# Attention and gated convolutional MLP on one core: the MLP starts two steps earlier, three weight pieces are converted beside it

## The chip, the cores and the metric

The kernel runs on one core of a Trainium2 chip. The time is that of one execution on the device in microseconds (us); a kernel's time is the median of its runs. The profile is one further execution, recorded by the hardware profiler. TensorE (PE) multiplies matrices, VectorE (DVE) and ScalarE (ACT) work elementwise and may read the accumulators in PSUM, GpSimd (POOL) works elementwise on SBUF alone, SyncE (SP) issues nearly all DMAs. Each engine takes its instructions in the order in which they stand.

## The reference, cut to what matters

```python
# q, k, v: (4, 8, 576, 64) float32; x after it: (4, 576, 512)
q_rot, k_rot = rotate(q), rotate(k)                 # rotary embedding
scores = scale * np.matmul(q_rot, k_rot.transpose(0, 1, 3, 2))
scores = scores - np.max(scores, axis=-1, keepdims=True)
attn = np.exp(scores)
attn = attn / (np.sum(attn, axis=-1, keepdims=True) + 1e-09)
x = heads side by side of np.matmul(attn, v)
h = np.maximum(x @ w_in, 0.0)                       # w_in (512, 1024) float64
conv_out[s] = conv_w[0] * h[s-1] + conv_w[1] * h[s] + conv_w[2] * h[s+1]
out = (h / (1 + np.exp(-conv_out))) @ w_out         # w_out (1024, 512) float64
```

## The kernel before

There are 16 pairs of heads (4 batches by 4 pairs) with five steps each (`STEPS`): pair p has the steps 5p to 5p+4, one for each block of 128 queries, the fifth for the 64 queries left over. For one step, written in this text as letters:

- **S**: the scores of 128 queries on PE (`emit_S`, L251), then two row maxima on DVE (L259) and two exponentials with their sums on ACT (L263).
- **T**: 16 transposes of the exponentials on PE (`emit_T`, L311), taken out of PSUM by two copies on ACT into `pt` (L189). **R** is the transpose of the last 128 keys (`emit_Trem`, L336), taken out by ACT or DVE (`evac`, L189 or L191). S4 and T4 are S and T of the fifth step, which is half as much work.
- **E**: once per pair and half of the sequence, 20 matmuls of `pt` with v on PE (`emit_E`, L367); ACT copies the result (L377), DVE multiplies by the reciprocal sums (L381), ACT and POOL split it into a high and a low part `xT` (L385, L386).

The MLP (MoE in the code) works on eight blocks of 288 tokens, two for each batch. **M1** (`emit_M1`, L400) is one of eight units per block, 12 matmuls of `xT` with the split weights `winh` and `winl` in PSUM tile `pm`; after it come relu on ACT (L408), three taps of the convolution (L412 and twice L414 on DVE), tanh on ACT (L420), the gate on DVE (L423), and the split into `g` on ACT and POOL (L431, L432). These follow their M1 after 2, 5, 7 and 9 ticks (`defer`, `tick`); a tick goes by after most PE units. **M2** (`emit_M2`, L478) is a quarter of the down projection of 128 tokens, six matmuls of `g` with `wouth` and `woutl`. M1 of a block needs `xT` of all four pairs of its batch, M2 needs `g`.

The weights arrive as float64 in 16 pieces of 128 by 512 (`load_w`, 512 KB each) and become two float32 parts (`conv_w_piece`, `to_f32`): absolute value on ACT (L496), clamp, shift, merge and sign on DVE (L499, L505, L508, L513), the high part on ACT (L556), the low part by four subtractions on POOL (L559). The rotary embedding runs on POOL (`rope`, L180 and L183), for q and k of each pair nine instructions each, and DVE turns its result into `qT` and `kT` (L224, L227).

Nothing is scheduled by a planner at run time: `emit` fills a table (`plan`) of steps and ranks by `at(step, rank, fn)` and another (`moe`) of MLP units per step, and then emits both step by step. `WIDE` is the step at which the MLP begins; before it the steps use the wide PSUM layout of three banks per score tile and no MLP tiles, and all weight pieces are spread evenly over them. At `WIDE` the pools change, and block 0 begins; blocks take `MB` = 10 steps each, with `room` as the share of a step that is given to them. After step 79 the attention is over; the last two blocks run in a tail of their own.

Of the kernel before, what the change touches and what calls it, by code (L numbers as in the profile page):

```python
# [20 lines left out]
def attention_moe_kernel(ctx, tc, q, k, v, w_in, conv_w, w_out, tab, tabx, out):  # L21
# [52 lines left out]
    late = {"tail": False, "short": False}  # L74
# [257 lines left out]
    def emit_Trem(p, first, num):  # L332
        ps = spare(128 * num)
        for u in range(num):
            x = ST[p, first + u].rearrange("p h k -> p (h k)")[:, 512:640]
            nc.tensor.transpose(ps[:, 128 * u:128 * u + 128], x, idf)  # L336
        after(lambda: evac("V", pt[:, 8, 128 * first:128 * (first + num)], ps))
# [52 lines left out]
    def emit_M1(blk, f):  # L390
# [18 lines left out]
        c = late["pc"].tile([128, HS], F32, tag="c", name="c")  # L409

        def conv():
            nc.vector.tensor_scalar(out=c, in0=r[:, j:j + HS], scalar1=cw[:, f:f + 1], scalar2=None, op0=ALU.mult)  # L412
            for e in (1, 2):
                nc.vector.scalar_tensor_tensor(  # L414
                    out=c, in0=r[:, j + e:j + e + HS], scalar=cw[:, 8 * e + f:8 * e + f + 1], in1=c,
                    op0=ALU.mult, op1=ALU.add,
                )
# [72 lines left out]
    def to_f32(pool, w64, w, n):  # L490
        w32 = w64.bitcast(I32).rearrange("p (n t) -> p n t", t=2)
        h, l = w32[:, :, 1], w32[:, :, 0]
        t = pool.tile([128, n], I32, tag="wt", name="wt", bufs=3)[0:w64.shape[0]]
# [23 lines left out]
        return first, clamp, second, third  # L517
# [11 lines left out]
    def load_w(i):  # L529
        if i >= len(WPIECES):  # L530
            return
        src, _, _, kk, c = WPIECES[i]
        t = late["ws"].tile([128, 512], I64, tag="w64", name="w64", bufs=4)
        nc.sync.dma_start(out=t, in_=src[kk * 128:kk * 128 + 128, c:c + 512])
        stage[i] = t

    def conv_w_piece(i):
# [3 lines left out]
        def first():  # L541
            box["w"] = late["ws"].tile([128, 512], F32, tag="wf", name="wf", bufs=3)
            box["s"] = to_f32(late["ws"], stage.pop(i), box["w"], 512)
            box["s"][0]()
# [5 lines left out]
        def third():  # L550
            box["s"][3]()
            load_w(i + 3)
# [18 lines left out]
    def conv_cw():  # L571
        t = stage.pop("cw")
        w = late["ws"].tile([32, 128], F32, tag="cwf", name="cwf", bufs=1)
        for fn in to_f32(late["ws"], t, w, 128):
            fn()
        stage["cwf"] = w
# [9 lines left out]

    late["ws"] = wctx.enter_context(tc.tile_pool(name="ws", bufs=2))
    wcv = [conv_w_piece(i) for i in range(len(WPIECES))]
    wsteps = [wcv[0][0]]
    for i in range(len(wcv)):  # L590
        wsteps += [wcv[i + 1][0]] if i + 1 < len(wcv) else []
        wsteps += wcv[i][1:]

    WIDE = 26
# [8 lines left out]
    def emit():  # L603
        with tc.manual_schedule(engines=engines):
# [25 lines left out]
            for p in range(NP):  # L630
# [10 lines left out]
                if n + 4 < WIDE:  # L641
# [15 lines left out]
            nw = len(wsteps)  # L657
            for i, u in enumerate(wsteps):
                x = (WIDE - 1) * i // nw
                at(x, 0.4, u)  # L660
# [17 lines left out]
            for n in range(max(max(plan), max(moe)) + 1):  # L678
                late["n"] = n
                late["short"] = n >= STEPS * NP - 3  # L680
                if n == WIDE:
# [5 lines left out]
                    late["po"] = ctx.enter_context(tc.tile_pool(name="po", bufs=1))  # L687
                    late["g"] = gpool.tile([128, 2, NF, RING], F32R, name="g")
# [100 lines left out]
```

## Time and profile before

| | us |
|---|---|
| median of 3 runs | 516.94 |
| lowest and highest run | 515.4, 518.79 |
| the profiled execution | 514.66 |
| its span, first to last instruction | 512.7 |
| PE busy in the span | 469.0 |
| DVE, ACT, POOL busy | 365.0, 311.8, 300.3 |

The profiled execution lies 2.28 us below the median. Busy time of PE is modelled at its ends, and matmuls are pipelined, so a busy PE can still hold small waits. In a list of instructions the columns are start, duration, engine, source line, operation, output and inputs, shapes, count, and in brackets the idle time before and what ended it.

### The profile page before, as it was taken

To read this page: it belongs to the slowest core of one execution; us is meant where nothing else is said; L and a number is where in the kernel's file an instruction comes from. 1 tells how busy PE (TensorE), PEld (TensorE's weight loads), DVE (VectorE), ACT (ScalarE), POOL (GpSimd) and SP (SyncE) were. 2 spreads that over 40 slices of the span, in tenths; PEclk is the share of its full clock that TensorE was granted. 3 is DMA by queue.
4 is the path that set the end of the run, shared out by engine and by line. 5 is a ranking of instruction groups with operands and counts; after the bars stand their busy time and mean duration, and the time that the engine had idled before them with its cause. 6 is when DMAs were issued, how large, how long until landed. Compare 5 with 4: busy or idle time off the path is not lost.

```text
span 512.7 us, 10801 instructions
## 1 busy us (share of the span) xinstructions
PE 469.0 (91%) x3880; PEld 350.0 (68%) x3880; DVE 365.0 (71%) x656; ACT 311.8 (61%) x821; POOL 300.3 (59%) x479
## 2 busy tenths in 40 slices
PE   1878789786999899999999999999999999999997
PEld 1445446553766587767878687868777676889986
DVE  5699889995597759684868487765868284748951
ACT  2588877885576767675667575754657564325520
POOL 3789988999576747646492829274573021314530
PEclk9999987997999999999999999999999999999999
DMA  8978965843424243433425251524220201000011
GB/s 225 178 128 165 191 158 140 188 113 76 88 47 94 47 93 68 93 69 73 90 49 90 63 100 45 88 73 88 51 68 1 68 1 46 22 21 22 1 42 60
DMA packets 139256, 42.61 MB, mean 83 GB/s; under 512 B 132012, under 2 KB 132804, under 8 KB 139204
## 3 DMA queue, kind: packets, MB, share of 16 engines
q1 hardware_dynamic: 137860, 41.54, 37.1%
q8 instruction: 30, 0.49, 0.4%
q10 hardware_dynamic: 1344, 0.39, 0.3%
q14 instruction: 22, 0.18, 0.1%
HBM read 37.12 MB, written 4.79 MB: 82 GB/s over the span
## 4 chain that ended last, share of the span: by engine, by line
PE 67%; DVE 13%; ACT 7%; POOL 5%; DMA 5%; issue 2%; SPq 0%; ACTq 0%; DVEq 0%; POOLq 0%
PE pm L400 13%; PE sp L251 12%; PE pm L478 11%; PE tp L367 11%; PE mt L478 8%; PE mt L400 5%; PE tp L311 5%; DVE negm L259 4%; ACT st L263 3%; ACT pt L189 2%; DMA rq<-q 2%; POOL rk L180 1%; DVE c L414 1%; POOL woutl L559 1%; DMA rk<-k 1%
## 5 line engine op out<-in xcount | busy, mean ns | idle before, releaser
L259 DVE TENSOR_REDUCE negm<-sp 128x1 f32<-128x576 f32 x144 | 102.4, 747 | 73.9 <-PE sp L251 66.6
L432 POOL TENSOR_TENSOR g<-c,g 128x288 fp32r<-128x288 f32 (+4 forms) x88 | 56.8, 658 | 154.6 <-ACT g L431 151.7
L189 ACT ACTIVATE pt<-tp 128x512 f32<-128x512 f32 (+3 forms) x176 | 84.4, 528 | 53.7 <-PE tp L311 53.3
L251 PE MATMUL sp<-kT,qT 64*128 64x288 f32 (+4 forms) x556 | 104.3, 474 | 6.4 <-DVE kT L227 3.2
L263 ACT ACTIVATE st<-sp,negm 128x576 f32<-128x576 f32 x128 | 94.0, 746 | 14.6 <-DVE negm L259 14.1
L400 PE MATMUL pm<-xT,winh 128*128 128x290 f32 x384 | 81.7, 305 | 0.0
L414 DVE SCALAR_TENSOR_TENSOR c<-rr,cw,c 128x288 f32<-128x288 f32 x128 | 77.6, 606 | 4.5
L251 PEld LDWEIGHTS sp<-kT,qT 64*128 64x128 f32 (+1 forms) x556 | 47.2, 179 | 33.5 <-issue 15.4
L478 PE MATMUL pm<-wouth,g 128*128 128x512 f32 x176 | 65.8, 415 | 0.0
L400 PEld LDWEIGHTS pm<-xT,winh 128*128 128x128 f32 x384 | 62.3, 189 | 3.2 <-issue 0.4
L311 PEld LDWEIGHTS tp<-idf,st 64*128 64x128 f32 x1024 | 42.5, 140 | 27.1 <-ACT st L263 16.2
L180 POOL TENSOR_TENSOR rq<-rq,tabt 128x192 f32<-128x192 f32 x90 | 56.8, 666 | 5.5 <-DMA rq<-q 5.3
L311 PE MATMUL tp<-idf,st 64*128 64x64 f32 x1024 | 49.4, 229 | 10.5 <-ACT st L263 10.4
L400 PE MATMUL pm<-xT,winl 128*128 128x290 f32 x192 | 56.7, 296 | 0.0
L367 PE MATMUL tp<-pt,vm 128*64 128x290 f32 x384 | 53.6, 422 | 3.4 <-ACT pt L189 3.4
L180 POOL TENSOR_TENSOR rk<-rk,tabt 128x192 f32<-128x192 f32 x90 | 56.6, 665 | 0.0
L423 DVE SCALAR_TENSOR_TENSOR c<-c,rr 128x288 f32<-128x288 f32 x64 | 36.6, 575 | 15.3 <-ACT c L420 15.3
L412 DVE TENSOR_SCALAR c<-rr,cw 128x288 f32<-128x288 f32 x64 | 33.3, 521 | 18.0 <-ACT rr L408 14.0
L386 POOL TENSOR_TENSOR xT<-xn,xT 128x290 fp32r<-128x290 f32 x32 | 29.6, 940 | 24.1 <-ACT xT L385 24.1
L367 PEld LDWEIGHTS tp<-pt,vm 128*64 128x64 f32 x384 | 27.0, 140 | 23.0 <-ACT pt L189 4.4
L420 ACT ACTIVATE c<-c 128x288 f32<-128x288 f32 x64 | 28.5, 445 | 17.7 <-DVE c L414 17.5
L478 PEld LDWEIGHTS pm<-wouth,g 128*128 128x128 f32 x176 | 33.0, 188 | 8.1
(102 smaller groups left out, 797.8 us busy)
## 6 DMA issues: line engine op xcount, KB each, us to landing
out<-ot SPq DMA_DIRECT2D x17, 256.0 KB
rq<-q SPq DMA_DIRECT2D x30, 144.0 KB
rq<-q SPq DMA_DIRECT2D x60, 72.0 KB
rk<-k SPq DMA_DIRECT2D x30, 144.0 KB
rk<-k SPq DMA_DIRECT2D x60, 72.0 KB
w<-moe_w_in SPq DMA_DIRECT2D x8, 512.0 KB
vm<-v SPq DMA_DIRECT2D x32, 128.0 KB
w<-moe_w_out SPq DMA_DIRECT2D x8, 512.0 KB
```

What stands on the lines that cost most here:

```text
L180: nc.gpsimd.tensor_tensor(out=y, in0=y, in1=tabt[:, a:a + 3], op=ALU.mult)
L189: nc.scalar.activation(out=out, in_=in_, func=AF.Copy, scale=1.0 if sc is None else sc)
L251: nc.tensor.matmul(out=out, lhsT=qt[64 * h:64 * h + 64, c], rhs=kt[64 * h:64 * h + 64, a:a + n], start=True, stop=True)
L259: reds.setdefault((p, s), []).append(lambda: nc.vector.tensor_reduce(out=nm, in_=sc, axis=AX.XY if len(sc.shape) == 3 else AX.X, op=ALU.ma ...
L263: lambda: nc.scalar.activation(out=dst, in_=sc, func=AF.Exp, bias=nm, scale=1.0, accum_out=sm)
L311: nc.tensor.transpose(ps[r][:, 64 * k:64 * k + 64], x[i], idf[i, i])
L367: nc.tensor.matmul(out=xp[64 * h:64 * h + 64, :], lhsT=vmain[p][:, h, i, :] if i < 4 else vrem[:, h, :], rhs=pt[:, 2 * i + h if i < 4 else ...
L400: nc.tensor.matmul(out=ps[:, 0:XW], lhsT=w[:, kk, fs], rhs=xT[:, xs, e, :], start=(i == 0), stop=(i == n - 1))
L414: nc.vector.scalar_tensor_tensor(out=c, in0=r[:, j + e:j + e + HS], scalar=cw[:, 8 * e + f:8 * e + f + 1], in1=c, op0=ALU.mult, op1=ALU.add,)
L423: nc.vector.scalar_tensor_tensor(out=c, in0=c, scalar=1.0, in1=r[:, j + 1:j + 1 + HS], op0=ALU.add, op1=ALU.mult)
L432: nc.gpsimd.tensor_tensor(out=lo, in0=c[:, o:o + n], in1=hi.bitcast(F32), op=ALU.subtract)
L478: nc.tensor.matmul(out=ops[tt][:, 0:width], lhsT=g_tile(tt, f, e), rhs=w[:, f, cols], start=(f == 0 and i == 0), stop=(f == NF - 1 and i = ...
```

## The change

`WIDE` goes from 26 to 24, so block 0 begins at step 24 and every later block two steps earlier. Only the first 13 weight pieces (`NWIDE`) are converted before it; the last three (rows 640 to 1023 of w_out) follow in the steps 26 to 34, one sub-step each, with one buffer for the raw piece and one for its conversion, and each load is issued when the piece before is done. The high parts of these are made from the conversion buffer itself. In block 0 the first tap of the convolution moves from DVE to ACT, directly behind relu, and until step 34 ACT takes the R transposes out of PSUM instead of DVE. MLP units of a block are sorted by their nominal place and then put at even distances by rank; a step with E counts as 0.62 of a step instead of 0.5, and as 1.3 in block 0.

```diff
@@ emit_Trem
-        after(lambda: evac("V", pt[:, 8, 128 * first:128 * (first + num)], ps))
+        after(lambda: evac("V" if late["n"] > WIDE + MB else "A", pt[:, 8, 128 * first:128 * (first + num)], ps))
@@ emit_M1
         c = late["pc"].tile([128, HS], F32, tag="c", name="c")
+        if blk == 0:
+            nc.scalar.activation(out=c, in_=r[:, j:j + HS], func=AF.Copy, scale=cw[:, f:f + 1])
         def conv():
-            nc.vector.tensor_scalar(out=c, in0=r[:, j:j + HS], scalar1=cw[:, f:f + 1], scalar2=None, op0=ALU.mult)
+            if blk:
+                nc.vector.tensor_scalar(out=c, in0=r[:, j:j + HS], scalar1=cw[:, f:f + 1], scalar2=None, op0=ALU.mult)
@@ to_f32, load_w, conv_w_piece
-        t = pool.tile([128, n], I32, tag="wt", name="wt", bufs=3)[0:w64.shape[0]]
+        t = pool.tile([128, n], I32, tag="wt", name="wt", bufs=late["wb"][1])[0:w64.shape[0]]
+        if w is None:
+            w = t.bitcast(F32)
-        t = late["ws"].tile([128, 512], I64, tag="w64", name="w64", bufs=4)
+        t = late["ws"].tile([128, 512], I64, tag="w64", name="w64", bufs=late["wb"][0])
-            load_w(i + 3)
+            load_w(i + late["wb"][2])
@@ emit
-    WIDE = 26
+    WIDE = 24
+    NWIDE = 13
-                if n + 4 < WIDE:
+                if n + 1 < WIDE:
                     for i in range(4):
                         at(n + 1 + i, 2, lambda p=p, i=i: emit_Trem(p, i, 1))
+            for k, u in enumerate(sum(wcv[NWIDE:], [])):
+                at(WIDE + 2 + k, 0.4, u)
-                room = [0.5 if n % STEPS == 0 and n < STEPS * NP + 2 else 1.0 for n in range(n0, n0 + MB)]
-                us = [(0.09 + 0.1 * f, lambda blk=blk, f=f: emit_M1(blk, f)) for f in range(NF)]
+                busy = 0.62 if blk else 1.3
+                room = [busy if n % STEPS == 0 and n < STEPS * NP + 2 else 1.0 for n in range(n0, n0 + MB)]
+                us = [((f + 0.5) / NF, lambda blk=blk, f=f: emit_M1(blk, f)) for f in range(NF)]
...
-                for x, u in us:
-                    y, k = x * sum(room), 0
+                us.sort(key=lambda e: e[0])
+                for i, (x, u) in enumerate(us):
+                    y, k = (i + 0.5) / len(us) * sum(room), 0
@@ emit, at step WIDE
+                    late["wb"] = (1, 1, 1)
+                    late["ws"] = ctx.enter_context(tc.tile_pool(name="ws2", bufs=1))
+                    load_w(NWIDE)
```

On POOL, before, from the rotary embedding of k of pair 5 to the first zeros for the relu tiles (`xT` in the fourth row is half 0 of pair 3, the last that M1 of block 0 needs; `rq` and `rk` below it are pair 6):

```order
L180 TENSOR_TENSOR rk<-rk,tabt 128x192 x6
L183 TENSOR_TENSOR rk<-rk 128x6x32 x3
L559 TENSOR_TENSOR woutl<-wf,wouth 128x128 x12
L386 TENSOR_TENSOR xT<-xn,xT 128x290
L180 TENSOR_TENSOR rq<-rq,tabt 128x192 x6
L183 TENSOR_TENSOR rq<-rq 128x6x32 x3
L559 TENSOR_TENSOR woutl<-wf,wouth 128x128 x4
L386 TENSOR_TENSOR xT<-xn,xT 128x290
L180 TENSOR_TENSOR rk<-rk,tabt 128x192 x6
L183 TENSOR_TENSOR rk<-rk 128x6x32 x3
L691 MEMSET rr_1702 128x1
```

The same place on POOL with the change:

```order
L566 TENSOR_TENSOR woutl<-wf,wouth 128x128 x4
L386 TENSOR_TENSOR xT<-xn,xT 128x290
L180 TENSOR_TENSOR rk<-rk,tabt 128x192 x6
L183 TENSOR_TENSOR rk<-rk 128x6x32 x3
L566 TENSOR_TENSOR woutl<-wf,wouth 128x128 x8
L386 TENSOR_TENSOR xT<-xn,xT 128x290
L705 MEMSET rr_1564 128x1
```

Two pieces stand between k of pair 5 and that `xT` instead of three, and the zeros stand ahead of pair 6 instead of behind it.

On PE, before, from the last matmuls of E of pair 4 on (`sp` is S, `tp<-idf,st` is T, the eight rows of `pm` are one M1):

```order
L367 MATMUL tp<-pt,vr 64x290 x2
L251 MATMUL sp<-kT,qT 128x288 x4
L311 MATMUL tp<-idf,st 128x64 x16
L400 MATMUL pm<-xT,winh 128x290 x2
L400 MATMUL pm<-xT,winl 128x290
L400 MATMUL pm<-xT,winh 128x290 x2
L400 MATMUL pm<-xT,winl 128x290
```

The same place on PE with the change:

```order
L367 MATMUL tp<-pt,vr 64x290 x2
L251 MATMUL sp<-kT,qT 128x288 x4
L311 MATMUL tp<-idf,st 128x64 x16
L251 MATMUL sp<-kT,qT 128x288 x4
L311 MATMUL tp<-idf,st 128x64 x16
L400 MATMUL pm<-xT,winh 128x290 x2
L400 MATMUL pm<-xT,winl 128x290
```

The M1 between the two score steps behind E has moved in front of E; step 26, and step 31 in the same way, hold no MLP unit.

On ACT with the change, around the conversion of the last piece (`wouth<-wt` is the high part of piece 14, `wt<-w_2091` the absolute value of piece 15, which overwrites the same buffer; ahead of them stands S of step 31):

```order
L434 ACTIVATE g<-c 128x288
L423 ACTIVATE c<-c 128x288
L263 ACTIVATE st,sums<-sp,negm 128x576 x2
L563 ACTIVATE wouth<-wt 128x512
L502 ACTIVATE wt<-w_2091 128x512
L189 ACTIVATE pt<-tp 128x8x64 x2
L263 ACTIVATE st,sums<-sp,negm 128x576 x2
```

On ACT before, at the step after the exponentials of a step of block 0:

```order
L420 ACTIVATE c<-c 128x288
L189 ACTIVATE pt<-tp 128x8x64 x2
L431 ACTIVATE g<-c 128x288
L263 ACTIVATE st,sums<-sp,negm 128x576 x2
L408 ACTIVATE rr_1704<-pm 128x289
```

The two conversions stand between the exponentials of one step and the copies and exponentials of the next, where ACT before had nothing of the weights.

## Rows read from the trace of the kernel before

**Rows 1.** Busy time by stretch: start:end, length, engines, granted PE clock, DMA share.

```profile
20.00:121.00 101.00, 81.02 (x839) 49.69 (x837) 92.27 (x151) 81.14 (x210) 96.73 (x149) 0.95 0.69 154
121.00:128.00 7.00, 6.42 (x34) 3.32 (x36) 2.74 (x6) 4.02 (x14) 7.00 (x14) 0.51 0.27 47
...
175.00:396.00 221.00, 218.01 (x1845) 166.95 (x1842) 155.32 (x286) 141.99 (x372) 129.02 (x206) 1.00 0.33 70
```

**Rows 2.** Chain that ended last, in order of time: start, us, what; 106 to 122 us.

```profile
115.17 4.20 POOL woutl L559 x8
```

**Rows 3.** POOL in order of time: start, duration, instructions; 80 to 123 us.

```profile
80.39 4.24 POOL L180 TENSOR_TENSOR rq<-rq,tabt 128x192 f32<-128x192 f32 x6
...
115.13 6.48 POOL L559 TENSOR_TENSOR woutl<-wf,wouth 128x128 fp32r<-128x128 f32 x12
121.56 1.01 POOL L386 TENSOR_TENSOR xT<-xn,xT 128x290 fp32r<-128x290 f32 x1
```

**Rows 4.** PE in order of time at the start of block 0.

```profile
122.38 4.14 PE L367 MATMUL tp<-pt,vm 128*64 128x290 f32 x16 [0.53 <-ACT pt L189]
126.30 1.18 PE L367 MATMUL tp<-pt,vr 128*64 128x290 f32 x4
...
129.24 0.54 PE L400 MATMUL pm<-xT,winh 128*128 128x290 f32 x2
...
131.06 2.17 PE L367 MATMUL tp<-pt,vm 128*64 128x290 f32 x16
133.06 0.66 PE L367 MATMUL tp<-pt,vr 128*64 128x290 f32 x4
```

**Rows 5.** Groups by line and shape: count, busy us, mean ns, idle before.

```profile
L508 DVE SCALAR_TENSOR_TENSOR wt<-w,wt 128x512 int32<-128x512 int32 x16 | 14.6, 913 | 0.5
L513 DVE SCALAR_TENSOR_TENSOR wf<-w,wt 128x512 int32<-128x512 int32 x16 | 13.9, 866 | 0.5
...
L496 ACT ACTIVATE wt<-w 128x512 f32<-128x512 f32 x16 | 11.0, 694 | 0.0
L505 DVE TENSOR_SCALAR wt<-wt 128x512 int32<-128x512 int32 x16 | 10.4, 648 | 0.6
...
L499 DVE TENSOR_SCALAR wt<-wt 128x512 f32<-128x512 f32 x16 | 8.8, 553 | 0.0
...
L556 ACT ACTIVATE wouth<-wf 128x512 fp32r<-128x512 f32 x8 | 5.1, 636 | 1.6 <-DVE wf L513 1.4
```

**Rows 6.** The same view: the first tap, tanh for a copy of that shape.

```profile
L412 DVE TENSOR_SCALAR c<-rr,cw 128x288 f32<-128x288 f32 x64 | 33.3, 521 | 18.0 <-ACT rr L408 14.0 <-POOL rr L691 4.0
...
L420 ACT ACTIVATE c<-c 128x288 f32<-128x288 f32 x64 | 28.5, 445 | 17.7 <-DVE c L414 17.5
```

**Rows 7.** The chain that ended last again: E of pair 6, an M2, an M1.

```profile
174.79 5.11 PE tp L367 x40
...
181.56 1.59 PE pm L478 x6
183.15 1.61 PE pm L400 x12
```

**Rows 8.** All engines in order of time, one step of block 1.

```profile
218.10 1.24 PE L251 MATMUL sp<-kT,qT 64*128 64x288 f32 x8
...
219.37 1.42 DVE L259 TENSOR_REDUCE negm<-sp 128x1 f32<-128x576 f32 x2 [1.24 <-PE sp L251]
219.76 0.50 PE L478 MATMUL pm<-wouth,g 128*128 128x512 f32 x1
...
221.88 0.75 ACT L263 ACTIVATE st<-sp,negm 128x576 f32<-128x576 f32 x1
```

**Rows 9.** Busy time by stretch: five steps with eight MLP units, no M1 beside E.

```profile
203.20:229.45 26.25, 25.26 (x219) 18.97 (x219) 20.58 (x38) 17.23 (x45) 15.15 (x23) 1.00 0.37 76
```

**Rows 10.** DMAs in the chain that ended last: start, us.

```profile
93.85 6.26 DMA vm<-v
...
103.73 2.38 DMA rd<-rt
```

More of the change, by code (lines that the diff above doesn't have):

```diff
@@ L73, in attention_moe_kernel @@
     ptp = ptctx.enter_context(tc.tile_pool(name="ptp", bufs=1, side="right"))
-    late = {"tail": False, "short": False}
+    late = {"tail": False, "short": False, "wb": (4, 3, 3)}
     pt = ptp.tile([128, 9, S], F32, name="pt")
@@ L515, in third @@
             )
-        return first, clamp, second, third
+        return first, clamp, second, third, w
     def bits(i):
@@ L529, in load_w @@
     def load_w(i):
-        if i >= len(WPIECES):
+        if i >= len(WPIECES) or (i >= NWIDE) != ("m" in psum):
             return
         src, _, _, kk, c = WPIECES[i]
-        t = late["ws"].tile([128, 512], I64, tag="w64", name="w64", bufs=4)
+        t = late["ws"].tile([128, 512], I64, tag="w64", name="w64", bufs=late["wb"][0])
         nc.sync.dma_start(out=t, in_=src[kk * 128:kk * 128 + 128, c:c + 512])
@@ L541, in first @@
         def first():
-            box["w"] = late["ws"].tile([128, 512], F32, tag="wf", name="wf", bufs=3)
-            box["s"] = to_f32(late["ws"], stage.pop(i), box["w"], 512)
+            w = late["ws"].tile([128, 512], F32, tag="wf", name="wf", bufs=3) if i < NWIDE else None
+            box["s"] = to_f32(late["ws"], stage.pop(i), w, 512)
+            box["w"] = box["s"][4]
             box["s"][0]()
@@ L573, in conv_cw @@
         w = late["ws"].tile([32, 128], F32, tag="cwf", name="cwf", bufs=1)
-        for fn in to_f32(late["ws"], t, w, 128):
+        for fn in to_f32(late["ws"], t, w, 128)[:4]:
             fn()
@@ L589, in attention_moe_kernel @@
     wsteps = [wcv[0][0]]
-    for i in range(len(wcv)):
-        wsteps += [wcv[i + 1][0]] if i + 1 < len(wcv) else []
+    for i in range(NWIDE):
+        wsteps += [wcv[i + 1][0]] if i + 1 < NWIDE else []
         wsteps += wcv[i][1:]
-    WIDE = 26
     MB = 10
@@ L656, in emit @@
                     at(n + (9 if j and n + 8 < WIDE else 8), 1.7 + j, lambda p=p, j=j: norms.pop((p, j))())
-            nw = len(wsteps)
             for i, u in enumerate(wsteps):
-                x = (WIDE - 1) * i // nw
-                at(x, 0.4, u)
+                at((WIDE - 1) * i // len(wsteps), 0.4, u)
+            for k, u in enumerate(sum(wcv[NWIDE:], [])):
+                at(WIDE + 2 + k, 0.4, u)
             at(12, 3, conv_cw)
@@ L670, in emit @@
                     ne = 4 if blk % 4 == 0 else 0
-                    us += [(0.05 * i if i < ne else 0.05 * ne + (1 - 0.05 * ne) * (i - ne) / (len(m2) - ne), u) for i, u in enumerate(m2)]
-                for x, u in us:
-                    y, k = x * sum(room), 0
+                    us += [(0.05 * i if i < ne else 0.05 * ne + (1 - 0.05 * ne) * (i - ne + 0.5) / (len(m2) - ne), u) for i, u in enumerate(m2)]
+                us.sort(key=lambda e: e[0])
+                for i, (x, u) in enumerate(us):
+                    y, k = (i + 0.5) / len(us) * sum(room), 0
                     while y >= room[k]:
```

## The prediction

> **What bounds the kernel now.** I read the busy time by stretch first, then the chain of waits, then each engine in order of time at the step where the MLP begins. The stretches show two regimes [rows 1]. From 20 to 121 us, before the MLP, PE is busy 81.0 of 101 us, DVE 92.3 and POOL 96.7: there the elementwise engines set the pace, by the weight conversion and the rotary embedding. From 175 to 396 us PE is busy 218.0 of 221 us, so an edit there can win 3 us at most; a step costs what its PE work costs. Between the two lies block 0, with M1 alone beside the attention. The chain of waits runs through POOL at the end of the first regime [rows 2]. In POOL's own order the stretch from the rotary embedding of q of pair 4 (80.39 us) to the end of the `xT` that M1 needs (121.56 + 1.01 = 122.57 us) has no gap worth counting and takes 42.2 us [rows 3].
>
> The third thing to see is what a step costs when PE has too little to do. In one step of block 1, S starts at 218.10 us, DVE's maxima at 219.37, and the second exponential ends at 222.63 [rows 8]. The next S needs those two score tiles, and may start some 0.2 us before the second is free: 4.3 us from S to S, whatever PE does meanwhile. S and T take PE 1.66 us of it (218.10 to 219.76, where an M2 starts) [rows 8]; an M1 takes 1.61 and an M2 1.59 [rows 7]. A step with both is bound by PE (4.9), a step with one waits, a step with none waits most.
>
> **The earlier start (term A).** Before, the first M1 (f0) starts at 129.24 us and ends at about 130.85 [rows 4, 7]. With the change its last quarter waits for `xT` of pair 3, half 0, behind POOL's chain. In the 42.2 us of that chain stands one weight piece fewer: four subtractions at 6.48 / 12 = 0.54 us, 2.2 us [rows 3]. The chain also starts earlier, since up to there DVE has converted one piece fewer: 0.553 + 0.648 + 0.913 + 0.866 = 2.98 us [rows 5]. As DVE is 91% busy, I take 2.5 of it; the ends are 0 and 2.98. So `xT` ends at 80.39 - 2.5 + 40.0 = 117.9 us and f0 at 118.3, 12.55 us sooner. PE itself would be there earlier and waits. Behind f0 now stand two S and T (3.3 us) and half an E, 2.00 + 0.66 = 2.66 us at full clock [rows 4], that stood in front of it: 6.0 us come back. A = -12.55 + 6.0 = **-6.6** (-4.1 to -7.0).
>
> **Block 0 (term B).** Before, 130.85 to the E of pair 6 at 174.79 us [rows 7] is 43.9 us. PE's work in it is nine S and T (14.9), three halves of E (8.0) and seven M1 (11.3), 34.2 us; R stands on both sides and is left out. So 9.7 us are lost. By the 4.3 us step, six steps with M1 lose 4.3 - 3.27 = 1.03 us each and a short one without a unit some 1.5, 7.7 in all; 2.0 us are other waits. With the change the same stretch holds eleven S and T (18.3), four halves of E (10.6), nine M1 (14.5; two of block 1) and one M2 (1.6). Two steps, 26 and 31, have no unit and lose 4.3 - 1.66 = 2.64 us each, five with M1 lose 1.03 each, and I keep the 2.0: 12.5 us. B = 12.5 - 9.7 = **+2.8** (+0.8 without the 2.0). The M1, M1 and M2 done early are in A and B as work that isn't left for later.
>
> **The three pieces beside it (term C).** Per piece DVE gets 2.98 us, ACT 0.69 + 0.64, POOL 2.2 [rows 3, 5]. As busy time this fits: DVE is also rid of eight first taps of 0.52 us and some R copies, for which ACT pays about what it pays for a tanh of that shape, 0.45 us a tap [rows 6]; I cost these moves at nothing, covered by the steps' waits, and at up to 1 us either way if that cover is gone. What counts is the order. With one buffer, ACT's absolute value of piece 14 stands two short `xT` splits behind the high part of piece 13, that of piece 15 directly behind the high part of piece 14; each must wait for the four subtractions (2.2 us) between, and for a load that is issued only when DVE has done the sign of the piece before. Behind it on ACT stand the copies of T and the exponentials, and for these wait R and the next S. The subtractions alone leave ACT idle for 2.2 - 0.9 = 1.3 and 2.2 us. Of each the step's own wait takes up 1.03: 3.5 - 2.06 = **+1.4**. The load of 512 KB isn't shown landing. It is bounded by 2.38 us, a DMA of some KB, and 6.26, one of 128 KB behind two weight pieces [rows 10]. Up to 2.8 us (0.64 + 2.2) it is hidden by the subtractions, and I take it there, since SP issues nothing large just ahead of it. At 6.26 the waits are 4.7 and 5.6 us, and C is 10.3 - 2.1 = +8.2. At the other end ACT's wait lies wholly beside PE's work and C is 0.
>
> The rows show a small DMA in the chain at 2.38 us [rows 10]. The Trainium skill (DMA: Bandwidth & Descriptors, Anatomy of one DMA) gives a fixed part of about 2.0 us and bytes over 436 GB/s, for DMAs issued by GpSimd; these go by SP. An estimate from that page is 3.2 us for a piece, 0.4 beyond what the subtractions hide, and by it C would be +2.2 and the sum 0.8 us higher. No row here shows a piece's landing, so that can't be told from the trace.
>
> **Placing by rank (term D).** Before, in the groups of five steps whose E has no M1 beside it, PE loses 26.25 - 25.26 = 0.99 us [rows 9]; there are four such groups. With the change every E has an M1 ahead of it, and that loss goes; but seven steps with two score tiles have an M2 alone. There ACT has less to do than in the step of rows 8, and I take 4.0 us from S to S: 4.0 - 1.66 - 1.59 = 0.75 each. D = 5.3 - 4.0 = **+1.3** (-4.0 if those steps don't wait, +3.4 at 4.3 us).
>
> **What stays.** Eight M1 and the M2 of each block remain, and the tail's order is the same. After the last E fewer units stand before the tail, seven and a half microseconds of them and four M2, against an `xT` chain of some 5 us: nothing.
>
> **Clock.** Between 121 and 128 us the granted clock is 0.51, the 1.2 GHz level; half an E takes 5.1 us (122.38 to 127.48) instead of 2.66 [rows 1, 4]. That lies before f0 in the kernel now and is in A. With the change PE waits in front of f0, and 0 to 2.4 us of it may return behind f0. I leave it out of the sum and hold it in the range.
>
> **The sum.** -6.6 + 2.8 + 1.4 + 1.3 = -1.1 us. From the profiled execution, 514.66, that is 513.6; from the median, 2.28 higher, 515.8. I forecast 515.0, that is, no difference that a measurement of this kernel can tell: about 1%, 5.2 us, is what it can tell from none.
>
> **The rivals.** *Faster:* the waits that I add don't arise. If ACT's wait for the conversions lies beside PE's work (C = 0), the 2.0 us of other waits in block 0 go, as the zeros for the relu tiles no longer come behind pair 6 on POOL (DVE waited 4.0 us for them [rows 6]), and the M2-only steps run at PE's pace (D = -4.0), the sum is -6.6 + 0.8 - 4.0 = -9.8: 505 by the profiled execution, 507 by the median. For it: ACT is idle 79 of 221 us later [rows 1], and DVE loses work at the right place. Against it: the loop from S to S is there in the rows, and two steps without a unit are new.
>
> *Slower:* the loads land late. One raw buffer means that no load is in flight while a piece is converted. At 6.26 us after issue ACT stands still for 4.7 and 5.6 us with the softmax behind it, and PE does half of the next E at 1.2 GHz: -6.6 + 2.8 + 8.2 + 1.3 + 2.4 = +8.1, 523 or 525. It passes 1% once what PE loses to the two waits and the clock together is over 7.7 us. For it: rows 10 hold such a landing. Against it: two weight pieces were queued ahead of that one.
>
> *It starts no earlier than POOL allows:* if POOL's chain starts no sooner (A = -4.1) and the clock falls in front of f0 (+2.4), the sum is +3.8, 518.5 or 520.7; the step number has moved and the time hardly.
>
> **How the numbers follow.** No difference: 0.45, of which 0.15 is the last rival. Faster by over 1%: 0.35. Slower by over 1%: 0.20. The range reaches from the first rival by the median, 507, to the lower figure of the second and a little on, 523.5; it leaves out the rest of both. The likeliest case alone has 510 to 520.
>
> **What would show it right or wrong.** Right: POOL's last `xT` for block 0 ends near 118 us and f0's last matmuls wait for it; PE waits some 2.6 us in the steps 26 and 31; ACT is idle 1 to 2 us before the absolute values of pieces 14 and 15; E of pair 6 starts near 176 us. Wrong: f0 done before 115 us (POOL was not the bound), ACT idle for 4 us or more before a conversion with DMA as the releaser (the load is the bound), or M2-only steps without idle on PE (the step is shorter than I read).

## The result, and the profile after

The change makes the kernel slower: 521.99 us (median of 7 runs, 520.64 to 523.65) against 518.10 (7 runs), a ratio of 1.0105 with a 95% interval of 1.0079 to 1.0131. The forecast was 515.0 and no difference. Executions of one kernel differ by some us (those of the kernel before ran from 515.4 to 519.55). The profiled execution took 520.64, its span 518.9 us, 6.2 more than before.

I cut both spans at the end of the first M1, f0, and at the start of the E of pair 6. Busy time of these stretches, first of the kernel before (start:end, length, busy us of PE with matmuls, PEld, DVE, ACT, POOL, then granted PE clock, DMA share, GB/s):

```profile
131.12:174.79 43.67, 39.91 (x357) 28.74 (x357) 34.36 (x63) 30.30 (x80) 26.26 (x46) 1.00 0.39 76
174.79:512.70 337.91, 329.25 (x2582) 260.60 (x2582) 224.21 (x416) 188.56 (x504) 159.04 (x252) 1.00 0.25 56
```

and of the changed kernel:

```profile
119.16:184.55 65.39, 57.12 (x451) 41.77 (x449) 43.38 (x73) 44.99 (x114) 37.88 (x58) 0.90 0.44 88
184.55:518.90 334.35, 329.63 (x2553) 256.69 (x2552) 226.96 (x414) 185.69 (x501) 163.68 (x254) 1.00 0.25 57
```

f0 ends 11.96 us sooner, block 0 takes 21.72 longer, the rest is 3.56 shorter: +6.2. The loss lies in block 0, and its clock is 0.90 where it was 1.00. POOL's last `xT` for f0, at 121.56 before [rows 3], ends in the changed kernel at 117.43, and the last quarter of f0, which needs it, starts on PE at 118.59 without having waited:

```profile
116.63 0.80 POOL L386 TENSOR_TENSOR xT<-xn,xT 128x290 fp32r<-128x290 f32 x1 [0.24 <-ACT xT L385]
```

```profile
118.59 0.44 PE L400 MATMUL pm<-xT,winh 128*128 128x290 f32 x2
```

Where PE waits in block 0, in order of time on PE:

```profile
127.89 1.24 PE L251 MATMUL sp<-kT,qT 64*128 64x288 f32 x8
...
132.17 2.53 PE L251 MATMUL sp<-kT,qT 64*128 64x288 f32 x7 [2.55 <-ACT st L263]
...
148.67 0.44 PE L336 MATMUL tp<-idf,st 128*128 128x128 f32 x2 [2.38 <-ACT pt L189]
...
165.40 2.08 PE L251 MATMUL sp<-kT,qT 64*128 64x288 f32 x7 [2.55 <-ACT st L263]
```

The first and the last wait are those of the steps 26 and 31, which have no unit. The middle one stands behind a conversion on ACT, as these rows of ACT show:

```profile
144.48 0.61 ACT L563 ACTIVATE wouth<-wt 128x512 fp32r<-128x512 f32 x1
145.00 0.76 ACT L385 ACTIVATE xT<-xn 128x290 fp32r<-128x290 f32 x2
147.47 0.67 ACT L502 ACTIVATE wt<-w 128x512 f32<-128x512 f32 x1 [1.71 <-POOL woutl L566]
148.04 1.06 ACT L189 ACTIVATE pt<-tp 128x512 f32<-128x512 f32 x2
...
165.95 0.64 ACT L563 ACTIVATE wouth<-wt 128x512 fp32r<-128x512 f32 x1
168.59 0.67 ACT L502 ACTIVATE wt<-w 128x512 f32<-128x512 f32 x1 [2.00 <-DMA w<-moe_w_out]
```

The prediction expected the two waits of the empty steps (2.64 us each) and ACT's two; for the middle wait of PE, 2.38 us, it had 0.3 us left. What it put at nothing is what follows each wait; stretches by pairs, a wait and then what comes behind it:

```profile
128.00:132.20 4.20, 1.65 (x25) 1.27 (x25) 2.11 (x3) 3.52 (x9) 2.45 (x5) 1.00 0.15 46
132.20:136.00 3.80, 3.80 (x25) 2.56 (x25) 1.54 (x3) 0.67 (x3) 0.00 (x0) 0.55 0.78 144
145.80:149.00 3.20, 0.82 (x6) 0.45 (x4) 0.88 (x2) 1.53 (x4) 3.16 (x5) 1.00 1.00 215
149.00:156.00 7.00, 7.00 (x33) 5.49 (x34) 5.09 (x8) 5.15 (x16) 4.89 (x7) 0.54 0.30 44
161.00:165.40 4.40, 1.85 (x26) 1.36 (x25) 2.80 (x4) 2.94 (x8) 4.40 (x8) 1.00 0.22 67
165.40:169.00 3.60, 3.60 (x25) 2.49 (x26) 1.76 (x3) 1.60 (x4) 3.05 (x7) 0.67 1.08 236
```

Behind each wait the granted clock is 0.54 to 0.67 on average, so for most of these stretches at the 1.2 GHz level, and PE is busy all the time. The seven matmuls of S at 132.17 take 2.53 us; in a kernel shown below (with spacing), behind the same wait but at a clock of 1.00, they take 1.72. (The 1.24 us at 127.89 are no measure for it: there S runs in one piece, here T runs in between.)

### The profile page after: what moved, and what is told of

The parts are those of the page before. It is cut to its first block, busy times and chain, and to the rows that moved or that the text cites. A ratio compares the mean times of both kernels' runs of the same rounds, so it can differ in the third digit from the quotient of the medians.

```text
span 518.9 us, 10782 instructions
## 1 busy us (share of the span) xinstructions
PE 476.4 (92%) x3882; PEld 353.3 (68%) x3882; DVE 364.4 (70%) x643; ACT 314.9 (61%) x833; POOL 301.6 (58%) x479
## 4 chain that ended last, share of the span: by engine, by line
PE 67%; DVE 12%; ACT 11%; DMA 4%; issue 2%; POOL 1%; SPq 1%; DVEq 0%; ACTq 0%; POOLq 0%
PE sp L251 13%; PE pm L400 13%; PE tp L367 12%; PE pm L481 10%; PE mt L481 7%; PE tp L311 6%; PE mt L400 5%; ACT pt L189 4%; ACT st L263 4%; DVE negm L259 4%; DVE wt L511 1%; DVE wt L505 1%; DMA rq<-q 1%; DVE wt L514 1%; DMA rd<-rt 1%
## 5 line engine op out<-in xcount | busy, mean ns | idle before, releaser
L435 POOL TENSOR_TENSOR g<-c,g 128x288 fp32r<-128x288 f32 (+4 forms) x88 | 54.7, 633 | 160.6 <-ACT g L434 123.8
L251 PE MATMUL sp<-kT,qT 64*128 64x288 f32 (+4 forms) x560 | 111.4, 482 | 7.1 <-ACT st L263 5.1
L417 DVE SCALAR_TENSOR_TENSOR c<-rr,cw,c 128x288 f32<-128x288 f32 x128 | 84.9, 663 | 17.2 <-ACT c L411 13.0
L400 PE MATMUL pm<-xT,winh 128*128 128x290 f32 x384 | 84.4, 313 | 0.0
L251 PEld LDWEIGHTS sp<-kT,qT 64*128 64x128 f32 (+1 forms) x560 | 50.2, 182 | 39.9 <-issue 13.1
L311 PEld LDWEIGHTS tp<-idf,st 64*128 64x128 f32 x1024 | 45.6, 142 | 31.5 <-ACT st L263 18.9
L311 PE MATMUL tp<-idf,st 64*128 64x64 f32 x1024 | 54.0, 233 | 13.9 <-ACT st L263 13.2
L400 PE MATMUL pm<-xT,winl 128*128 128x290 f32 x192 | 57.5, 300 | 0.0
L426 DVE SCALAR_TENSOR_TENSOR c<-c,rr 128x288 f32<-128x288 f32 x64 | 39.0, 609 | 24.6 <-ACT c L423 24.6
L367 PE MATMUL tp<-pt,vm 128*64 128x290 f32 (+1 forms) x400 | 53.0, 407 | 0.3 <-ACT pt L189 0.3
L400 PEld LDWEIGHTS pm<-xT,winl 128*128 128x128 f32 x192 | 37.4, 195 | 0.0
```

The source lines that it names most:

```text
L251: nc.tensor.matmul(out=out, lhsT=qt[64 * h:64 * h + 64, c], rhs=kt[64 * h:64 * h + 64, a:a + n], start=True, stop=True)
L311: nc.tensor.transpose(ps[r][:, 64 * k:64 * k + 64], x[i], idf[i, i])
L367: nc.tensor.matmul(out=xp[64 * h:64 * h + 64, :], lhsT=vmain[p][:, h, i, :] if i < 4 else vrem[:, h, :], rhs=pt[:, 2 * i + h if i < 4 else ...
L400: nc.tensor.matmul(out=ps[:, 0:XW], lhsT=w[:, kk, fs], rhs=xT[:, xs, e, :], start=(i == 0), stop=(i == n - 1))
L417: nc.vector.scalar_tensor_tensor(out=c, in0=r[:, j + e:j + e + HS], scalar=cw[:, 8 * e + f:8 * e + f + 1], in1=c, op0=ALU.mult, op1=ALU.add,)
L426: nc.vector.scalar_tensor_tensor(out=c, in0=c, scalar=1.0, in1=r[:, j + 1:j + 1 + HS], op0=ALU.add, op1=ALU.mult)
```

## Experiments

The stretch ahead of f0 differs between executions by several us without any edit in it (f0 ended between 118.4 and 126.0 us), and each profile is one execution, so differences of 1 us between two profiles are not told from none. Mechanisms are read from the stretches behind f0: (a) from its end to the S of step 26, (b) from there to the E of pair 6, with the mean granted clock of (b), and (c) to the end.

| kernel | a | b | clock in b | c | ratio to before, 95% interval |
|---|---|---|---|---|---|
| the change | 8.73 | 56.66 | 0.88 | 334.35 | 1.0105 (1.0079 to 1.0131) |
| even placing | 7.46 | 57.18 | 0.88 | 334.35 | 1.0116 (1.0060 to 1.0171) |
| two buffers | 8.73 | 56.33 | 0.91 | 334.28 | 1.0086 (1.0056 to 1.0115) |
| filler | 8.72 | 55.43 | 0.94 | 334.33 | 1.0083 (1.0048 to 1.0119) |
| taps on DVE | 8.38 | 55.85 | 0.91 | 334.30 | 1.0069 (1.0031 to 1.0106) |
| spacing | 13.09 | 49.45 | 1.00 | 334.48 | 1.0101 (1.0044 to 1.0158) |
| spacing, buffers, taps | 12.84 | 49.84 | 0.93 | 334.35 | 1.0063 (1.0033 to 1.0092) |
| the same and filler | 10.69 | 47.53 | 1.00 | 334.24 | 0.9981 (0.9954 to 1.0008) |
| the same and even | 13.14 | 44.95 | 1.00 | 334.46 | 0.9960 (0.9937 to 0.9983) |
| all 16 pieces first | 8.67 | 50.25 | 0.93 | 334.33 | 1.0098 (1.0064 to 1.0132) |
| spacing from 26, even | 7.46 | 47.89 | 1.00 | 334.38 | 0.9901 (0.9870 to 0.9932) |
| the same, buffers, taps | 7.13 | 47.06 | 1.00 | 334.29 | 0.9881 (0.9850 to 0.9911) |

In the kernels with even placing one M1 (1.6 us) stands in b instead of a.

### One cause at a time: four edits that change little

**Even placing.**

```diff
-                busy = 0.62 if blk else 1.3
+                busy = 0.62
```

> One number is put back: in block 0 a step with E counts as 0.62 of a step as in the other blocks, not as 1.3. The eight M1 then stand in the steps 24, 26 to 29 and 31 to 33, so the steps 26 and 31 each have one, and the steps 25 and 30 with the second halves and the E of pair 5 have none. The kernel with the change needs 65.5 us from the end of the first M1 (119.05) to the E of pair 6 (184.55). Theory 1, the steps without a unit are what costs, by their wait and by the clock that stands at 0.55 and 0.67 right behind them: both stretches go, and the 65.5 become about 61 to 62 (some 1.6 us of wait and as much again of clock for each of the two places, less 1 for S and T behind an E that now has no M1 before it); ratio to the kernel before about 1.003. Theory 2, the conversions on ACT and POOL hold everything up: the stretch stays within 1 us of 65.5 and the ratio at 1.0105. Theory 3, the softmax loop sets the pace whatever stands beside it: the waits only move to other steps, 64 to 65.5, ratio 1.008 to 1.0105.

Measured: a and b together 64.64 instead of 65.39, ratio 1.0116, as theories 2 and 3 had it. PE's waits in the steps 26 and 31 went, and ACT's wait before piece 15 grew from 2.00 to 4.25 us, on ACT:

```profile
164.69 0.61 ACT L563 ACTIVATE wouth<-wt 128x512 fp32r<-128x512 f32 x1
169.56 0.66 ACT L502 ACTIVATE wt<-w 128x512 f32<-128x512 f32 x1 [4.25 <-POOL woutl L566]
```

Why POOL is late is seen in POOL's order of the same run:

```profile
161.01 4.03 POOL L180 TENSOR_TENSOR rk<-rk,tabt 128x192 f32<-128x192 f32 x6
165.00 1.91 POOL L183 TENSOR_TENSOR rk<-rk 128x192 f32<-128x192 f32 x3
166.87 1.00 POOL L435 TENSOR_TENSOR g<-c,g 128x288 fp32r<-128x288 f32 x1
167.84 1.69 POOL L566 TENSOR_TENSOR woutl<-wt,wouth 128x128 fp32r<-128x128 f32 x4
```

The high part was there at 165.30, but the four subtractions that free the one conversion buffer stand behind 5.9 us of rotary embedding. In this run piece 15 is anchored there.

**Two conversion buffers.**

```diff
-                    late["wb"] = (1, 1, 1)
+                    late["wb"] = (1, 2, 1)
```

> One number is changed: the three pieces beside block 0 get two buffers for the conversion, with one for the raw piece as before. The absolute value of piece 14 then need not wait for the four subtractions of piece 13 on POOL (ACT idle 1.71 us there with the change), and that of piece 15 waits for its load alone (2.00 us idle there, load landing 3.9 us after issue). Theory 2, conversions: the wait of 1.7 us goes, the R that stood behind it on PE no longer waits 2.4, the clock does not fall to 0.54 from 149 to 156 us, and the 65.5 us become 61 to 63; ratio 1.002 to 1.006. Theory 1, steps without a unit: the 1.7 us are hidden anyway, 65 to 65.5, ratio 1.0105. If the load is the real bound of piece 14 too, ACT waits there for the DMA instead, and nothing is won.

Measured: b 56.33. The wait on POOL before piece 14 turned into a wait for the load, as the last sentence of the expectation allowed, on ACT:

```profile
148.27 0.66 ACT L502 ACTIVATE wt<-w 128x512 f32<-128x512 f32 x1 [1.11 <-DMA w<-moe_w_out]
```

Its load was issued at 144.68. Two limits stood at the same place, and removing one shows the other.

**Filler.**

```diff
+            def filler():
+                ps = m_tile()
+                for i in range(3 * NK):
+                    nc.tensor.matmul(out=ps[:, 0:XW], lhsT=winh[:, i % NK, 0:128],
+                        rhs=xT[:, xslot[0, i % NK, 0], 0, :], start=(i == 0), stop=(i == 3 * NK - 1))
+            for n in (WIDE + 2, WIDE + 7):
+                moe.setdefault(n, []).append((0, filler))
```

> Twelve matmuls of the shape of an M1 are added at the end of each of the steps 26 and 31, in a PSUM tile that nobody reads; the rest is the kernel with the change, so PE has 2 x 1.6 us more to do and no result changes. They stand where PE waits 2.5 us for the exponentials. Theory 1 in its clock part: PE is busy through the two waits, the granted clock does not fall to 0.55 and 0.67 behind them, and although work was added the stretch from the first M1 to the E of pair 6 gets shorter, from 65.5 to 62 to 64 us; ratio 1.004 to 1.008. If the clock is not what costs: the filler lies inside the waits and the stretch stays at 65.5, or it grows by up to 3.2 us where it doesn't fit, ratio 1.0105 to 1.017.

Measured: 24 matmuls more, and b is 1.23 us shorter, not longer; a and b together take 64.15. That is the direction of the clock theory, but just outside its 62 to 64. In step 26 it did what was expected: the clock stayed at 1.00, and from the S behind the wait to the next S it took 4.63 us instead of 5.83. Behind step 31 the gain was lost again: ACT's wait before piece 15 grew to 2.99 us.

**Taps on DVE.**

```diff
-        if blk == 0:
-            nc.scalar.activation(out=c, in_=r[:, j:j + HS], func=AF.Copy, scale=cw[:, f:f + 1])
...
-            if blk:
-                nc.vector.tensor_scalar(out=c, in0=r[:, j:j + HS], scalar1=cw[:, f:f + 1], scalar2=None, op0=ALU.mult)
+            nc.vector.tensor_scalar(out=c, in0=r[:, j:j + HS], scalar1=cw[:, f:f + 1], scalar2=None, op0=ALU.mult)
```

> The first taps of block 0 go back from ACT to DVE, the R copies stay on ACT. ACT then has eight instructions of some 0.45 us less, DVE eight of 0.52 us more; the wait of DVE for the first tap behind relu on ACT (13.0 us idle in all, five times, the longest 4.1) goes. Theory 4, the taps on ACT delay the softmax: the stretch of 65.5 us loses 2 to 4 us, ratio 1.003 to 1.007. Rival, DVE is the engine that needs relief beside the conversions: it grows by 1 to 3 us, ratio 1.013 to 1.016. If neither engine ends the waits by these: within 1 us, 1.0105.

Measured: a and b 64.23, 1.2 us less than with the change, between "within 1 us" and the 2 to 4 of theory 4; the ratio, 1.0069, is theory 4's, but its interval reaches past 1.0105. At the S behind the empty step 31 this run was 4.2 us ahead of the change, counted from f0, and lost 3.1 of it again behind ACT's wait of 3.72 us for POOL before piece 15.

### The conversions apart from the rest

**Spacing:** the sub-steps move to the steps 25 to 27, 29 to 31 and 33 to 35.

```diff
-                at(WIDE + 2 + k, 0.4, u)
+                at(WIDE + 1 + k + k // 3, 0.4, u)
```

> Only the steps of the three late pieces move: they begin in step 25 instead of 26, and one step is left free between two pieces (25 to 27, 29 to 31, 33 to 35 instead of 26 to 34 without a gap). Buffers stay single. The absolute value of the next piece is then due two steps, some 9 us, after the sign that lets its load be issued, and some 8 us after the high part. Theory 2, the conversions anchor block 0 (in the two runs in which the rest of block 0 was faster, the wait of ACT before piece 15 only grew, from 2.0 to 3.7 and 4.3 us, and its time stayed near 168): ACT waits under 0.5 us before pieces 14 and 15, the 65.4 us from the first M1 to the E of pair 6 become 59 to 62, ratio 0.998 to 1.004. Theory 1, the steps without a unit and the clock behind them: 64 to 65.5, ratio 1.008 to 1.011. If piece 15 comes too late for the M2 of block 0 that needs it, a new wait of PE appears in the steps 36 and 37.

Measured: a and b together 62.54, short of theory 2's 59 to 62, and a ratio of 1.0101, theory 1's figure; but b falls from 56.66 to 49.45, with the same 380 or so matmuls. PE's busy time there falls from 48.49 to 42.79, and its idle time from 8.17 to 6.66. The changed kernel's b:

```profile
127.89:184.55 56.66, 48.49 (x381) 36.06 (x379) 37.66 (x63) 39.34 (x98) 29.15 (x45) 0.88 0.41 81
```

With spacing:

```profile
133.97:183.42 49.45, 42.79 (x380) 31.52 (x378) 38.56 (x62) 38.08 (x96) 28.39 (x42) 1.00 0.45 88
```

So b is 7.2 us shorter, 1.5 of it idle time of PE and 5.7 busy time. Not all of this is shown to be the conversions' doing. The two empty steps still wait 2.55 us each, but in this execution the clock stays at 1.00 behind them:

```profile
138.26 1.72 PE L251 MATMUL sp<-kT,qT 64*128 64x288 f32 x7 [2.55 <-ACT st L263]
...
142.67 1.60 PE L251 MATMUL sp<-kT,qT 64*128 64x288 f32 x7
```

From the S behind such a wait to the next S this kernel takes 4.41 and 4.43 us, where the change took 5.83 and 5.95: 2.9 of the 7.2 us. The next kernel with this spacing has such a fall again, so the spacing alone doesn't decide it. The ratio hardly moved, because I also began a step earlier, and there ACT waits for the load of piece 13, and stretch a grows by 4.4 us; the profiled execution is also the fastest of the four runs (519.76, the others 520.88 to 523.38). The issue on SP's queue and the wait on ACT in this run:

```profile
122.71 0.50 SPq L540 DMA_DIRECT2D w<-moe_w_out  x1
```

```profile
126.34 0.66 ACT L502 ACTIVATE wt<-w 128x512 f32<-128x512 f32 x1 [4.08 <-DMA w<-moe_w_out]
```

**All 16 pieces first.**

```diff
-    NWIDE = 13
+    NWIDE = 16
```

> All 16 pieces are converted before step 24 again, the rest is the kernel with the change (start at step 24, taps and R on ACT, placing by rank). No ACT wait for a conversion is left in block 0. The first M1 comes later: three pieces more on DVE (2.98 us each) and POOL (2.2 us each), 6.5 to 9 us, so it ends near 126 to 128 us instead of 119.2. From there to the E of pair 6 theory 2 expects 57 to 60 us instead of 65.4, and theory 1 63 to 65. Sum by theory 2: the E of pair 6 at 184 to 187, ratio 1.008 to 1.014; by theory 1: 190 to 192, ratio 1.02 to 1.025.

Measured: f0 ends at 125.05, a and b together take 58.92, the ratio is 1.0098: theory 2's figures, but for a somewhat earlier f0. Its b:

```profile
133.72:183.97 50.25, 44.19 (x381) 34.03 (x379) 32.62 (x53) 35.94 (x93) 25.59 (x39) 0.93 0.36 70
```

Here the steps behind the two empty ones take what they take with the change (5.89 and 5.88 us), so this is the fair comparison for the three pieces: 6.4 us in b, 4.3 of it PE's busy time for the same 381 matmuls and 2.1 its idle time. Of these 6.4 us, 5.3 lie around piece 14, from the S of the fifth step of pair 5 to the S behind the next E (142.64 to 161.12 with the change, 148.02 to 161.20 here). What the pieces cost beside block 0 is about what they cost ahead of it (f0 5.9 us later, within the spread of f0 above). Moving them bought nothing in these executions.

### With the spacing, the empty steps count

**Spacing, two conversion buffers, taps on DVE** (the three edits above together):

> The same spacing, with two buffers for the conversion and with the first taps of block 0 back on DVE; R copies stay on ACT. Theory 2: beyond what the spacing alone brings, the four subtractions on POOL can't hold ACT any more, and ACT is rid of 8 x 0.45 us: 1 to 2 us less than with the spacing alone, ratio 0.996 to 1.002. If the waits for conversions are gone with the spacing already, and the taps lay beside the softmax loop, it equals the spacing alone within 1 us.

Measured: b 49.84, the same as with spacing alone, and a ratio of 1.0063, above the 0.996 to 1.002 expected; but this execution isn't like that one: the clock fell once more, behind the empty step 26, and from the S there to the next it took 7.11 us instead of 4.41. Buffers and taps may be worth some 2 us that this fall hides; that isn't shown, and the last pair of kernels below puts them at 1.2. PE in order of time:

```profile
138.30 2.53 PE L251 MATMUL sp<-kT,qT 64*128 64x288 f32 x7 [2.55 <-ACT st L263]
...
145.41 1.24 PE L251 MATMUL sp<-kT,qT 64*128 64x288 f32 x8
```

**The same and filler:**

> As the run with the spacing from step 25, two conversion buffers and taps on DVE (62.7 us from the first M1 to the E of pair 6), with twelve matmuls of the shape of an M1 added at the end of the empty steps 26 and 31, whose result nobody reads. There the even placing brought 62.7 down to 58.1. If the clock behind the empty steps is the larger part of these 4.6 us, the filler brings 2 to 4 us although no useful work moves; if it is the wait itself, it brings nothing (62 to 63.5 us). A clean split: the rest, 58.1 against the filler's figure, is what the moved M1 are worth as work.

The same two S, with the filler (L689) ahead of the first:

```profile
133.80 1.89 PE L689 MATMUL pm<-xT,winh 128*128 128x290 f32 x12
136.42 1.71 PE L251 MATMUL sp<-kT,qT 64*128 64x288 f32 x7 [0.74 <-ACT st L263]
...
141.04 1.71 PE L251 MATMUL sp<-kT,qT 64*128 64x288 f32 x7
```

The clock from S to S, without the filler:

```profile
138.30:140.00 1.70, 1.70 (x6) 1.47 (x8) 1.09 (x2) 0.67 (x2) 0.00 (x0) 0.50 0.00 0
140.00:145.40 5.40, 5.40 (x35) 4.85 (x32) 2.45 (x4) 2.63 (x7) 0.00 (x0) 0.54 0.88 178
```

and with it:

```profile
136.40:141.00 4.60, 4.47 (x38) 3.50 (x38) 3.47 (x6) 2.84 (x8) 0.65 (x1) 1.00 0.53 100
```

From S to S 7.11 us without and 4.62 with the filler, while the S before the first of them lies 4.29 us ahead in both. Matmuls whose result nobody reads made b 2.3 us shorter (49.84 to 47.53), within the 2 to 4 expected of the clock; the 2.2 us less in a (10.69 against 12.84) lie ahead of the filler and are not its doing. The ratio went from 1.0063 to 0.9981, and the two intervals don't meet. The fall of the clock behind this empty step cost 2.5 us, as much as the wait; behind the same step of the changed kernel it cost 1.2 (5.83 against 4.63 with its filler).

**The same and even placing** (no filler):

> As the run before this one, and the M1 of block 0 stand as with 0.62 for a step with E, so that the steps 26 and 31 have one each. With the waits for conversions gone, the steps without a unit are what is left: theory 1 gives 2 to 4 us less than the run before this one (two waits of 1.6 us and the clock behind them), ratio 0.990 to 0.997. If the softmax loop sets the pace in any case, the two agree within 1 us.

Measured: b 44.95 although it holds one M1 more, ratio 0.996. The edit that was worth next to nothing alone (0.75 us) is worth 4.6 us (62.68 to 58.09 for a and b) once the conversions no longer wait. The filler, which moves no work, brought 2.3 of that in b; that its a and b come to 58.22 is due to the 2.2 us in a that aren't its doing. So half of the 4.6 us is the clock, and the rest the wait and the work moved into it.

**The spacing from step 26 on,** with all of this (pieces in 26 to 28, 30 to 32, 34 to 36):

```diff
-                at(WIDE + 2 + k, 0.4, u)
+                at(WIDE + 2 + k + k // 3, 0.4, u)
```

> As the run with spacing, two conversion buffers, taps on DVE and even placing, but piece 13 stays where the change had it: the pieces stand in the steps 26 to 28, 30 to 32 and 34 to 36. In that run ACT waited 4.05 us in step 25 for the load of piece 13, PE 4.21 us behind it, and a half of E then took 4.75 us at 1.2 GHz instead of 2.5. With the load two steps away this goes: 4 to 6 us less, the E of pair 6 at 173 to 175 instead of 179.1, ratio 0.984 to 0.989. If piece 15 now comes too late for the M2 that needs it, PE waits in the steps 36 to 38 and 1 to 4 us of it are given back. If something else held the start of block 0, the ratio stays near 0.996.

Measured: 511.51 us, ratio 0.9881, better than both kernels; no wait for piece 15 appears. The E of pair 6 starts at 178.01 in the profile, later than expected, as f0 ended 2.8 us later in this execution than in the one before; a and b take 54.19. Its b:

```profile
130.95:178.01 47.06, 44.29 (x393) 33.39 (x391) 40.39 (x70) 36.02 (x93) 30.05 (x45) 1.00 0.46 99
```

**The same with the single buffer and taps on ACT:**

> As the run before this one, but with a single conversion buffer and the first taps of block 0 on ACT, as in the change: only the spacing and the placing of block 0 differ from the changed kernel. If the waits came from the spacing and the empty steps alone, it agrees with the run before this one within 1 us (ratio 0.984 to 0.990). If the single buffer or the taps on ACT cost something of their own, it is 1 to 4 us slower.

Measured: 0.9901, 1.2 us more in a and b (55.35 against 54.19); the intervals overlap. Two edited lines, spacing and placing, carry the gain. This kernel also differs from the first experiment, even placing alone, by the spacing and nothing else. The b of that one, and then of this:

```profile
129.27:186.45 57.18, 49.63 (x392) 36.85 (x390) 38.99 (x67) 40.29 (x101) 30.06 (x46) 0.88 0.41 82
133.43:181.32 47.89, 45.01 (x393) 33.12 (x391) 37.96 (x63) 39.42 (x100) 29.39 (x45) 1.00 0.45 97
```

With no long wait at the steps 26 and 31 in either, the crowded conversions cost 9.3 us, half of it idle time of PE (7.55 against 2.88 us) and half busy time; the ratio is 1.0116 against 0.9901.

### Placing by rank

**The old placing from block 1 on.**

```diff
-                busy = 0.62 if blk else 1.3
+                busy = 0.5 if blk else 1.3
-                us = [((f + 0.5) / NF, lambda blk=blk, f=f: emit_M1(blk, f)) for f in range(NF)]
+                us = [(0.09 + 0.1 * f if blk else (f + 0.5) / NF, lambda blk=blk, f=f: emit_M1(blk, f)) for f in range(NF)]
...
-                us.sort(key=lambda e: e[0])
+                if not blk:
+                    us.sort(key=lambda e: e[0])
...
-                    y, k = (i + 0.5) / len(us) * sum(room), 0
+                    y, k = ((i + 0.5) / len(us) if not blk else x) * sum(room), 0
```

> The changed kernel with the old placing of the units from block 1 on (0.5 for a step with E, the old nominal places, no ranks); block 0 and all else as in the change. The kernel with the change needs 334.35 us from the E of pair 6 to the end, the kernel before 337.9 with one M1, one M1 and an M2 more to do (4.8 us). The prediction put placing by rank at +1.3 us: the old placing then takes some 333 us from there. If the placing is worth nothing, 334.4; if it is a gain that block 0 hides, 336 to 338.

Measured: 344.59 us from the E of pair 6 to the end instead of 334.35, ratio 1.026 (1.0219 to 1.0302), outside every figure on record. PE's largest waits in that stretch (waiting line, releaser, us in total, times, longest):

```profile
PE sp L251 <- ACT st L263: 8.8, 4, 2.9
```

With the start at 24 the blocks begin one step ahead of an E instead of one behind it, and the old places leave PE waiting there: all four of these waits stand before the S of a fifth step (232.58, 288.39, 346.57 and 408.52), the last step before an E. Placing by rank repairs a loss that the earlier start would bring, 10.2 us, and that is not seen in a comparison with the kernel before.

## Why the prediction was wrong, step by step

- **A, the earlier start: the time held, its mechanism did not.** `xT` ended at 117.43 (forecast 117.9), f0 at 119.16 (118.3). 11.96 us sooner, less the 6.0 that come back, is -6.0 where I had -6.6. But f0's last matmuls did not wait for POOL, as I had named for a sign: PE came to f0 at 117.27, behind E, S4 and T4, and its last quarter began 1.16 us after `xT` was there. In POOL's chain two errors cancelled: it began 1.03 us sooner (79.36 instead of 80.39), not 2.5, and took 4.1 us less, not 2.2. That the sum fits is in part luck, also because f0 ends anywhere from 118.4 to 126.0 us in executions of the experiments.
- **D, placing by rank: held.** From the E of pair 6 the changed kernel is 3.56 us shorter and has 4.8 less to do, so D is +1.25 (forecast +1.3). PE's idle time there falls from 8.66 to 4.72 us; against that the steps with an M2 alone wait as forecast, but hidden in busy time, since S and T run interleaved and wait for each other: behind an M2 alone they take 2.38 us (225.64 to 228.02) instead of 1.67 (222.01 to 223.68), 0.71 where I had 0.75. The groups of S and T of the kernel before from the E of pair 6 on:

```profile
L251 PE MATMUL sp<-kT,qT 64*128 64x288 f32 (+1 forms) x352 | 55.1, 426 | 0.0
L311 PE MATMUL tp<-idf,st 64*128 64x64 f32 x576 | 24.2, 223 | 0.0
```

and of the changed one, with the same counts 7.5 us more:

```profile
L251 PE MATMUL sp<-kT,qT 64*128 64x288 f32 (+1 forms) x352 | 59.3, 428 | 0.5
L311 PE MATMUL tp<-idf,st 64*128 64x64 f32 x576 | 27.5, 225 | 0.0
```

- **B and C, block 0: failed.** Together they were +4.2; measured, 21.72 less the 10.8 of work that moved in is +10.9. Without the conversions beside it block 0 took 58.92 (all 16 first), near the 57.5 of B, so B was 1.4 too low; the empty steps themselves took the 4.3 us that it forecast (4.28), but the step behind each took 5.89 and 5.88 us at the lower clock, where B had 4.3 too; the other parts of B were 1.8 too high. The three pieces cost 6.4 us like for like, and 9.3 with even placing, where C said 1.4.
- **The step of C that failed** is not the size of ACT's waits. ACT idled 1.71 and 2.00 us before pieces 14 and 15, forecast 1.3 and 2.2. It is the price put on them: "Of each the step's own wait takes up 1.03", and on the clock, "I leave it out of the sum and hold it in the range". The overlap failed at piece 14: its wait, priced at 0.3 us, left PE idle for 2.38 us in front of R, and behind that the clock stood at 0.57 from 149.04 to 157.00. That place holds 5.3 of the 6.4 us. I looked for the clock only in front of f0. The slower rival had one fall of 2.4 us, on an E, behind loads that land 6.26 us after issue. Its total, 523 by the profiled execution, is near the 520.64 measured, but that is luck: the loads did not land so late, and ACT stood still for 1.71 and 2.00 us, not for 4.7 and 5.6.
- **The load** lands 3.6 to 4.0 us after issue (ACT, waiting for it, went on 3.63 us after the issue with spacing, 3.59 with two buffers, 4.03 before piece 15 with the change; once, with spacing and even placing, 5.01), not within the 2.8 that I took, so it ends together with the subtractions (168.46 and 168.59 before piece 15 with the change). The Trainium skill (DMA: Bandwidth & Descriptors, Anatomy of one DMA) gave an estimate of 3.2 us for it; the traces are 0.4 to 0.8 above it (1.8 for the one of 5.01), for DMAs issued by SP where the page fits those of GpSimd.
- **POOL's order** I did not read for block 0. In three of the five kernels whose pieces follow each other without a gap (even placing, filler, taps on DVE) the rotary embedding ahead of the subtractions holds piece 15 until 165.6 to 169.6 us, and what went faster before it is lost there. With the change itself the load ends 0.13 us behind the subtractions. With two buffers piece 15 needs only those of piece 13, which were long done, and its load, issued at 165.83, is the likelier end of its wait at 169.78.

What stays open: which wait lowers the clock. Behind the same 2.55 us wait in step 26 the clock stood at 1.00 in the execution with spacing, and at 0.50 to 0.54 in the next kernel; with taps on DVE it stood at 1.00 behind a wait of 1.95 us in front of the R that was followed by 0.54 with the change (there 2.38 us). That a wait lowers the clock in one execution and not in another may be part of the spread of these kernels' times; no run here shows it.

## What to carry to other kernels

Price a new wait of the engine that sets the pace twice: once for its length, and once for the clock behind it, which here cost from nothing to as much again and appears as busy time. When work is moved beside a stage with few buffers, read the order of every engine in the chain that frees the buffer, and leave a step between two users of it. An edit that measures nothing alone can be worth 1% once another wait is gone, so undo causes in pairs before dropping a theory.

## What the runs showed of the hardware

Matmuls without any use, put where PE would have waited, made a stretch 2.3 us shorter (49.84 to 47.53), as the granted clock then stayed at its upper level. With the clock at 0.50 to 0.54 behind a wait of 2.55 us, seven matmuls of S took 2.53 us; behind the same wait in another execution, at 1.00, they took 1.72. The clock fell behind idle times of PE of 2.38 and 2.55 us, and stayed at 1.00 behind the same 2.55 us in another execution.
